# One pool for the four 4 MiB buffers at the end of a decode-attention kernel

## The chip, the cores and the metric

One core of a Trainium2 chip. The metric is the device time of one execution in microseconds (us). The kernel before takes 1310.4 us (median of 4 executions, 1310.23 to 1310.52). The profile of one execution spans 1308.8 us; its times count from the start of that span. A run on one core has no second die to be compared with; every profiled run here counts as undisturbed ("fast").

## The reference, cut to what matters

```python
# A: one decode step of attention.   B, D = 8, 576;  H, Sk, Dh = 32, 4096, 128
q = (x @ wq).reshape(B, 1, H, Dh).transpose(0, 2, 1, 3)
scores = einsum("bhqd,bhkd->bhqk", q, k_cache) * Dh ** -0.5      # k_cache: 256 MiB in bf16
o = einsum("bhqk,bhkd->bhqd", softmax(scores), v_cache)          # v_cache: 256 MiB in bf16
a = o.transpose(0, 2, 1, 3).reshape(B, 1, H * Dh) @ wo
# B: layernorm, 576 -> 4608 -> 576 MLP with gelu, small.   g = sigmoid((x * gate_w).sum(-1))
return g * a + (1 - g) * b
```

All of K and V has to be read once. That and some 20 MB of weights make 557 MB.

## The kernel before, where the change touches it

The work is cut into NG = 64 groups of 4 heads and one batch row. For each group VectorE multiplies K by q, TensorE sums the products to scores, and after the softmax TensorE multiplies the weights by V (the PV product); ScalarE then copies (evicts) that product from TensorE's accumulators, and two small groups of matmuls, gather and total, add up its parts and the softmax sums. A group needs one K tile and one V tile of 4 MiB, each 128 partitions of 128 key positions by 128 elements. K has two buffers, V has two; a tile of group g goes into buffer g % 2 when the tile of g - 2 has been used. The tiles below are named by group: K 62, V 63 and so on; V 63 is the last and comes in seven pieces. All loads are issued in order by one queue, SP, which stops at a load that has to wait.

```python
KB = [sb(f"KB{i}", [128, NTT, DH], BF16) for i in range(2)]
VB = [sb(f"VB{i}", [128, NTT, DH], BF16) for i in range(2)]
...
def load_k(g):                       # waits for the last VectorE product with K of group g - 2
    s = g % 2
    nK[s] += 1
    src = kv_src(A_k_cache, g)
    k_land[g] = op("sync", lambda e: e.dma_start(KB[s][:, :, :], src), [k_done.get(g - 2)], dma=(sK[s], 16 * nK[s]))
# load_v(g): the same with VB, v_done: the PV product of group g - 2 on TensorE
V_LAST = (32, 32, 16, 16, 16, 8, 8)
def load_v_pieces(g):                # V 63, piece by piece, each with its own semaphore
    ...
    t = load("sync", dst, part, f"sVl{n}", [v_done.get(g - 2)])
...
for g in range(NG):
    if 1 <= g <= NG - 3:
        load_k(g + 1)
    if 1 <= g <= NG - 2 and g != NG - 3:
        load_v(g)
    def between(c, g=g):             # called between the four score chunks of group g
        if c == 1 and g >= 1:
            rowsum(g - 1)
            if g < NG - 1:
                ...
            else:                    # group 63
                pv(NG - 3, 0, 1)     # PV of group 61: 32 matmuls
                evict(NG - 3)
                load_v_pieces(g)     # V 63 goes where V 61 was
        ...
        if c == 3:
            if 1 <= g < NG - 2:
                pv(g - 1, 0, 1)
                evict(g - 1)
    scores(g, between)               # VectorE products with K, TensorE sums, VectorE reductions
    if g == NG - 3:
        load_k(g + 2)                # K 63, after K 61 has been used
        load_v(g)
    ...
    softmax(g)
# after the loop: PV of 62, then PV of 63 piece by piece, normalisation, output projection, output
```

## Time and profile before

| what | value | view |
|---|---|---|
| DMA, mean over the span | 426 GB/s | the page, DMA packets |
| DMA share of the chain that ended last | 69% | the page, part 4 |
| VectorE, TensorE busy | 66%, 64% | the page, part 1 |
| V 63 issued | 1289.53 us | timeline of the SP queue |
| last data landed | 1304.68 us | chain in order of time |

Three lines of the page, each slice 32.7 us long: the mean busy share of the 16 DMA engines in tenths, what they moved, and the whole.

```profile
DMA  9999999999999999999999999999999999999997
GB/s 398 422 431 432 431 432 431 432 431 430 434 424 432 430 431 429 428 418 432 429 431 429 431 431 431 431 432 430 432 430 431 431 431 429 432 431 432 429 420 311
DMA packets 25255, 557.77 MB, mean 426 GB/s; under 512 B 2528, under 2 KB 6640, under 8 KB 7536
```

The kernel streams at about 431 GB/s in most slices. The end is the only slice that falls far short, and the last 4 us of it are the tail of arithmetic after the last byte. The windows view of the end (busy time of the engines by stretch; the last three columns are TensorE's granted clock, the DMA share and GB/s) shows a hole before that tail:

```profile
1280.00:1284.00 4.00, 1.40 (x4) 0.58 (x5) 3.97 (x4) 2.30 (x4) 0.00 (x0) 0.76 1.03 442
1284.00:1288.00 4.00, 4.00 (x22) 1.45 (x24) 3.38 (x4) 0.00 (x0) 0.00 (x0) 0.81 0.91 393
1288.00:1292.00 4.00, 3.61 (x38) 1.37 (x31) 4.00 (x4) 0.60 (x1) 0.00 (x0) 1.00 0.66 256
1292.00:1296.00 4.00, 3.67 (x40) 2.18 (x42) 2.26 (x9) 0.38 (x1) 0.00 (x0) 1.00 0.96 395
1296.00:1300.00 4.00, 2.84 (x53) 2.32 (x45) 0.69 (x1) 2.52 (x5) 0.00 (x0) 0.90 0.99 395
1300.00:1304.00 4.00, 3.35 (x85) 3.16 (x85) 0.54 (x3) 0.00 (x0) 0.00 (x0) 0.50 0.64 245
```

The waits of the SP queue (total us, times, longest us) name the cause, and its timeline gives the moments. The first two lines are the ordinary waits for a buffer, through the whole kernel; the third is the one before V 63:

```profile
SPq L223 <- DVE p L354: 950.5, 60, 26.3
SPq L229 <- PE psb L346: 215.1, 58, 4.2
...
SPq L187 <- PE psb L414: 28.8, 1, 28.8
```

```profile
1236.99 19.95 SPq L223 DMA_DIRECT2D KB<-in_A_k_cache_dram  x2
1256.98 3.77 SPq L229 DMA_DIRECT2D VB<-in_A_v_cache_dram  x2
1289.53 3.77 SPq L187 DMA_DIRECT2D VB<-in_A_v_cache_dram  x7
```

The reader sees K 62 and K 63 (issued 20 us apart), V 61 and V 62, and then 28.8 us in which the queue waits for the PV product of group 61 (L414) before it may issue V 63. The chain in order of time ends with the landing of V 63 and a short tail:

```profile
1292.80 11.88 DMA VB<-in_A_v_cache_dram
1304.68 0.05 issue
1304.72 0.39 PE psb L508 x8
1305.11 0.02 issue
1305.14 0.19 DVE OT_sb L517
```

The page does not show what each of the 16 DMA engines does, but the trace can be read for it. It holds 16 landing records for each of these loads, read here as one for each engine (the prediction below says on what ground). This table is worked out from those records (us; "7th" and "8th" in order of landing). The records do not name the engines: "the last engine" is the one that lands last.

```
kernel before   first     7th      8th      last    spread
first K tile      -        -        -        -       0.52
K 62           1256.56  1258.23  1263.59  1264.74    8.18
K 63           1268.16  1268.90  1273.31  1274.46    6.30
V 61           1277.87  1278.61  1283.02  1284.17    6.30
V 62           1287.58  1288.32  1292.71  1294.69    7.11
V 63, piece 1  1294.25  1294.73  1295.20  1297.15    2.90
V 63, piece 7  1302.09  1302.56  1302.77  1304.68    2.58
```

Seven engines are ahead and nine are behind. Those ahead land a tile every 9.71 us unless nothing has been issued; so do those behind, except that the last one needed 10.5 us for V 62. What an engine still has queued is called its ring below; an engine with nothing queued has run dry. From V 62 to the end the first engine takes 14.5 us and the last 10.0 us.

### The profile page before, as it was taken

The numbers are of one execution on the slowest core, as the hardware profiler recorded it, in microseconds if no ns is written. First come the engines' busy times: TensorE is split into PE (matmuls) and PEld (weight loads), VectorE is DVE, ScalarE is ACT, GpSimd is POOL, SyncE is SP. The second block draws the span as 40 slices with busy tenths as digits, with TensorE's granted clock in tenths as the row PEclk, the third lists the DMA queues.
The fourth block names the chain that finished last, engine by engine and source line by source line (L and its number), as shares of the span: only waits on it lengthen the run. The fifth ranks groups of instructions, "written<-read, shape, count | busy, mean of one in ns | idle before, by whom it ended". The sixth has DMA issues, their size and how long they took to land.

```text
span 1308.8 us, 12641 instructions
## 1 busy us (share of the span) xinstructions
PE 843.5 (64%) x5428; PEld 384.4 (29%) x5428; DVE 869.7 (66%) x1061; ACT 204.1 (16%) x393; POOL 2.5 (0%) x13
## 2 busy tenths in 40 slices
PE   3567766766746666646766766765766665766766
PEld 1223433433312233212322222322322222322323
DVE  4576676676747667646766766766776666776675
ACT  1201111111210110101011111011111111111111
POOL 0000000000000000000000000000000000000000
PEclk8878888878868888768878878878878878878878
DMA  9999999999999999999999999999999999999997
GB/s 398 422 431 432 431 432 431 432 431 430 434 424 432 430 431 429 428 418 432 429 431 429 431 431 431 431 432 430 432 430 431 431 431 429 432 431 432 429 420 311
DMA packets 25255, 557.77 MB, mean 426 GB/s; under 512 B 2528, under 2 KB 6640, under 8 KB 7536
## 3 DMA queue, kind: packets, MB, share of 16 engines
q1 hardware_dynamic: 24944, 556.95, 99.4%
q8 instruction: 42, 0.69, 0.2%
q14 instruction: 13, 0.11, 0.0%
q10 hardware_dynamic: 256, 0.03, 0.0%
HBM read 556.96 MB, written 0.01 MB: 426 GB/s over the span
## 4 chain that ended last, share of the span: by engine, by line
DMA 69%; DVE 20%; PE 10%; SPq 0%; issue 0%; ACT 0%
DMA KB<-in_A_k_cache_dram 68%; DVE p L354 16%; PE psb L364 10%; DVE s_sb L369 3%; DMA VB<-in_A_v_cache_dram 1%; SPq L187 0%; PE psb L414 0%; ACT L467 0%; SPq L229 0%; DVE mA L387 0%; SPq L223 0%; PE psb L477 0%; DVE mB L389 0%; ACT O_sb L427 0%; DVE gm L390 0%
## 5 line engine op out<-in xcount | busy, mean ns | idle before, releaser
L364 PE MATMUL psb<-p,ident 128*128 128x512 bf16 x2048 | 610.9, 459 | 412.2 <-DVE p L354 411.8
L354 DVE TENSOR_TENSOR p<-KB,q_bc 128x4096 bf16<-128x4096 bf16 x256 | 579.6, 2285 | 278.0 <-DMA KB<-in_A_k_cache_dram 278.0
L364 PEld LDWEIGHTS psb<-p,ident 128*128 128x128 bf16 x2048 | 218.1, 114 | 744.5 <-DVE p L354 445.2
L369 DVE TENSOR_REDUCE s_sb<-psb 128x32 f32<-128x512 f32 x256 | 176.1, 688 | 129.9 <-PE psb L364 129.6
L427 ACT ACTIVATE O_sb<-psb 128x512 f32<-128x512 f32 x63 | 37.6, 597 | 1032.2 <-PE psb L414 1032.2
L396 ACT ACTIVATE P<-s_sb,mD 32x128 bf16<-32x128 f32 x256 | 147.0, 574 | 12.9 <-DVE mD L393 9.0
L414 PE MATMUL psb<-VB,P 128*16 128x512 bf16 x2016 | 119.9, 379 | 0.3 <-DMA VB<-in_A_v_cache_dram 0.3
L432 PE MATMUL psb<-sel,O_sb 128*128 128x4 f32 x504 | 66.9, 256 | 32.9 <-ACT O_sb L427 32.9
L432 PEld LDWEIGHTS psb<-sel,O_sb 128*128 128x128 f32 x504 | 61.6, 192 | 41.3 <-ACT O_sb L427 41.2
L414 PEld LDWEIGHTS psb<-VB,P 128*16 128x16 bf16 x2016 | 44.7, 89 | 70.4 <-issue 26.3
L402 DVE TENSOR_REDUCE rs<-P 128x4 f32<-128x512 bf16 x64 | 43.5, 680 | 2.1 <-ACT P L396 2.1
L421 PEld LDWEIGHTS psb<-rs,ones 128*128 128x128 f32 x128 | 24.4, 192 | 9.3 <-issue 0.4
L348 ACT ACTIVATE q_bc<-psb 128x128 bf16<-128x128 f32 x64 | 17.4, 272 | 32.7 <-PE psb L346 32.7
L452 PEld LDWEIGHTS psb<-yT_sb,RB 128*128 128x128 bf16 (+1 forms) x216 | 19.4, 165 | 3.4
L452 PE MATMUL psb<-yT_sb,RB 128*128 128x8 bf16 (+1 forms) x216 | 19.8, 227 | 0.0
L387 DVE TENSOR_REDUCE mA<-s_sb 128x1 f32<-128x128 f32 x64 | 18.3, 286 | 2.2
L421 PE MATMUL psb<-rs,ones 128*128 128x4 f32 x128 | 18.4, 214 | 0.0
L389 DVE STREAM_TRANSPOSE mB<-mA 128x32 f32<-128x32 f32 x64 | 13.6, 213 | 2.2
L393 DVE STREAM_TRANSPOSE mD<-mC 128x32 f32<-128x32 f32 x64 | 13.6, 212 | 2.2
L346 PE MATMUL psb<-Q,Sel 128*128 128x128 bf16 x64 | 14.7, 229 | 0.0
L346 PEld LDWEIGHTS psb<-Q,Sel 128*128 128x128 bf16 x64 | 6.1, 96 | 27.0 <-issue 26.8
L390 DVE TENSOR_REDUCE gm<-mB 128x1 f32<-128x32 f32 x64 | 11.9, 186 | 2.2
(63 smaller groups left out, 84.7 us busy)
## 6 DMA issues: line engine op xcount, KB each, us to landing
KB<-in_A_k_cache_dram SPq DMA_DIRECT2D x64, 4096.0 KB, 27.2
VB<-in_A_v_cache_dram SPq DMA_DIRECT2D x63, 4096.0 KB, 33.1
RB<-in_B_w_dram SPq DMA_DIRECT2D x1, 5184.0 KB, 44.3
RB<-in_B_w_dram SPq DMA_DIRECT2D x1, 4608.0 KB, 36.6
RB<-in_A_wo_dram SPq DMA_DIRECT2D x1, 4608.0 KB, 44.7
RB<-in_A_wq_dram SPq DMA_DIRECT2D x1, 4096.0 KB, 12.8
VB<-in_A_v_cache_dram SPq DMA_DIRECT2D x2, 1024.0 KB, 8.7
VB<-in_A_v_cache_dram SPq DMA_DIRECT2D x3, 512.0 KB, 11.2
```

Of the source, the lines that this page charges most:

```text
L346: t = op("tensor", lambda e: e.matmul(qb_ps[:, 0:DH], lhsT=Sel[:, b, :], rhs=Q4[:, hg * DH:(hg + 1) * DH], start=True, stop=True), [a_Q[hg ...
L354: v_mult[g, c] = op("vector", lambda e: e.tensor_tensor(out=p1[:, par, :, :], in0=KB[s][:, c * CT:(c + 1) * CT, :], in1=qb, op=ALU.mult), ...
L364: p_sum[g, c] = op("tensor", lambda e, r=r, n=n: e.matmul(tr_ps[par][:, :], lhsT=ident[:, :], rhs=r, start=(n == 0), stop=(n == NCH - 1)), w)
L369: v_red[g, c] = op("vector", lambda e: e.tensor_reduce(out=s_sb[:, s, c * CT:(c + 1) * CT], in_=tr_ps[par][:, :].rearrange("p (t c) -> p t ...
L387: t = op("vector", lambda e: e.tensor_reduce(out=mA[:, 0:1], in_=s_sb[:, s, :], axis=AX.X, op=ALU.max), [v_red[g, NCK - 1], c_mA])
L396: a_exp[g] = op("scalar", lambda e, h=h, q=q: e.activation(out=P[q, s, :, h], in_=s_sb[q, s, :], func=ACT.Exp, bias=mD[q, s, 0:1], scale=1.0),
L402: v_rs[g] = op("vector", lambda e: e.tensor_reduce(out=rs[:, s, :], in_=P[:, s, :, :].rearrange("p t h -> p h t"), axis=AX.X, op=ALU.add), ...
L414: p_pv[g] = op("tensor", lambda e, o=o, tq=tq: e.matmul(o, lhsT=P[:, s, tq * TQ:(tq + 1) * TQ, :].rearrange("p t h -> p (t h)"), rhs=VB[s] ...
L421: p_z[g] = op("tensor", lambda e: e.matmul(oz_ps[:, HB:2 * HB], lhsT=ones[:, :], rhs=rs[:, g % 2, :], start=True, stop=True), [v_rs[g], v_ ...
L427: a_ev[g] = op("scalar", lambda e: e.activation(out=O_sb[:].rearrange("p t d -> p (t d)"), in_=o_ps[s][:, :], func=ACT.Copy), [p_pv[g], p_ ...
L432: p_oz[g] = op("tensor", lambda e, tt=tt: e.matmul(oz_ps[:, 0:HB], lhsT=O_sb[:, tt, :], rhs=sel16[:, tt, :], start=(tt == 0), stop=(tt == ...
L452: st["p_up"] = op("tensor", lambda e, w=w, o=o, kt=kt: e.matmul(o, lhsT=w, rhs=yT_sb[:, kt, :], start=(kt == 0), stop=(kt >= NKF)), [*ld_w ...
```

## The change

Its intent: no transfer near the end should wait for a late product. The four buffers become one pool. K 63 goes where V 59 was, V 61 where K 61 was, and V 63 where K 62 was, whichever came free first. The order of the loads stays; the PV product of group 61 no longer holds back V 63 and moves on TensorE behind all score sums of group 63.

```diff
-    KB = [sb(f"KB{i}", [128, NTT, DH], BF16) for i in range(2)]
-    VB = [sb(f"VB{i}", [128, NTT, DH], BF16) for i in range(2)]
+    KV = [sb(f"KV{i}", [128, NTT, DH], BF16) for i in range(4)]
...
+    k_slot = {g: g % 2 for g in range(NG)}
+    v_slot = {g: 2 + g % 2 for g in range(NG)}
+    k_slot[NG - 1], v_slot[NG - 3], v_slot[NG - 1] = 3, 1, 0
+    free = [None] * 4
...
+    def load_tile(cache, g, i):
+        nS[i] += 1
+        src = kv_src(cache, g)
+        return op("sync", lambda e: e.dma_start(KV[i][:, :, :], src), [free[i]], dma=(sS[i], 16 * nS[i]))
...     (all uses of KB, VB, k_done, v_done become KV, k_slot, v_slot, free)
     for g in range(NG):
         if 1 <= g <= NG - 3:
             load_k(g + 1)
+        if g == NG - 3:
+            load_k(g + 2)
+        if g == NG - 1:
+            load_v_pieces(g)
...
-                else:
-                    pv(NG - 3, 0, 1)
-                    evict(NG - 3)
-                    load_v_pieces(g)
...
             if c == 3:
+                if g == NG - 1:
+                    pv(g - 2, 0, 1)
+                    evict(g - 2)
...
         if g == NG - 3:
-            load_k(g + 2)
             load_v(g)
```

More of the change, by code (lines that the diff above doesn't have):

```diff
@@ L180, in bass_gated_mix__mha_block_cached__mixer_channel_mlp__decode_kernel @@
     YT_COL = 64
-    sK = [nc.alloc_semaphore(f"sK{i}") for i in range(2)]
-    sV = [nc.alloc_semaphore(f"sV{i}") for i in range(2)]
-    nK, nV = [0, 0], [0, 0]
+    sS = [nc.alloc_semaphore(f"sS{i}") for i in range(4)]
+    nS = [0] * 4
+    k_slot = {g: g % 2 for g in range(NG)}
+    v_slot = {g: 2 + g % 2 for g in range(NG)}
+    k_slot[NG - 1], v_slot[NG - 3], v_slot[NG - 1] = 3, 1, 0
+    free = [None] * 4
     def load(engine, dst, src, name, waits=()):
@@ L214, in kv_src @@
         return cache[b, hg * HB:(hg + 1) * HB].rearrange("h (p t) d -> (h p) t d", p=32)
-    k_done, v_done = {}, {}
     k_land, v_land = {}, {}
+    def load_tile(cache, g, i):
+        nS[i] += 1
+        src = kv_src(cache, g)
+        return op("sync", lambda e: e.dma_start(KV[i][:, :, :], src), [free[i]], dma=(sS[i], 16 * nS[i]))
     def load_k(g):
-        s = g % 2
-        nK[s] += 1
-        src = kv_src(A_k_cache, g)
-        k_land[g] = op("sync", lambda e: e.dma_start(KB[s][:, :, :], src), [k_done.get(g - 2)], dma=(sK[s], 16 * nK[s]))
+        k_land[g] = load_tile(A_k_cache, g, k_slot[g])
     def load_v(g):
-        s = g % 2
-        nV[s] += 1
-        src = kv_src(A_v_cache, g)
-        t = op("sync", lambda e: e.dma_start(VB[s][:, :, :], src), [v_done.get(g - 2)], dma=(sV[s], 16 * nV[s]))
-        v_land[g] = [(t, 0, NTT)]
+        v_land[g] = [(load_tile(A_v_cache, g, v_slot[g]), 0, NTT)]
     V_LAST = (32, 32, 16, 16, 16, 8, 8)
     def load_v_pieces(g):
-        s = g % 2
+        i = v_slot[g]
         src = kv_src(A_v_cache, g)
@@ L239, in load_v_pieces @@
         for n, nt in enumerate(V_LAST):
-            dst, part = VB[s][:, t0:t0 + nt, :], src[:, t0:t0 + nt, :]
-            t = load("sync", dst, part, f"sVl{n}", [v_done.get(g - 2)])
+            dst, part = KV[i][:, t0:t0 + nt, :], src[:, t0:t0 + nt, :]
+            t = load("sync", dst, part, f"sVl{n}", [free[i]])
             v_land[g].append((t, t0, t0 + nt))
@@ L354, in mult @@
         v_mult[g, c] = op("vector", lambda e: e.tensor_tensor(
-            out=p1[:, par, :, :], in0=KB[s][:, c * CT:(c + 1) * CT, :], in1=qb, op=ALU.mult),
+            out=p1[:, par, :, :], in0=KV[k_slot[g]][:, c * CT:(c + 1) * CT, :], in1=qb, op=ALU.mult),
             [k_land[g], a_qb[g], p_sum.get((g, c - 2) if c >= 2 else (g - 1, c + NCK - 2))]
@@ L358, in mult @@
         if c == NCK - 1:
-            k_done[g] = v_mult[g, c]
+            free[k_slot[g]] = v_mult[g, c]
         for n in range(NCH):
@@ L415, in pv @@
                     o, lhsT=P[:, s, tq * TQ:(tq + 1) * TQ, :].rearrange("p t h -> p (t h)"),
-                    rhs=VB[s][:, tq * TQ:(tq + 1) * TQ, :].rearrange("p t d -> p (t d)"),
+                    rhs=KV[v_slot[g]][:, tq * TQ:(tq + 1) * TQ, :].rearrange("p t d -> p (t d)"),
                     start=(tq < 4), stop=(tq >= NTQ - 4)), w)
-        v_done[g] = p_pv[g]
+        free[v_slot[g]] = p_pv[g]
     def total(g):
@@ L508, in pv_turned @@
                 p_oz[g] = op("tensor", lambda e, t=t: e.matmul(
-                    o_ps[s][:, 0:HB], lhsT=VB[s][:, t, :], rhs=P[:, s, t, :], start=(t == 0), stop=(t == NTT - 1)),
+                    o_ps[s][:, 0:HB], lhsT=KV[v_slot[g]][:, t, :], rhs=P[:, s, t, :], start=(t == 0), stop=(t == NTT - 1)),
                     [land, a_exp[g], a_ev.get(g - 2)] if t == t0 else ())
```

## The prediction

> **What bounds the kernel.** The sixteen DMA engines: the page's slices show DMA at 9 tenths or more in 39 of 40 slices, 426 GB/s on average over the 1308.8 us span; the chain of waits is 69% DMA. A 4 MiB tile takes 9.71 us (8 packets of 32 KB per engine, 1.215 us each). VectorE (66%) and TensorE (64%) have room.
>
> **What the change is after.** In the windows view DMA falls to 393 and 256 GB/s between 1284 and 1292 us. The SP queue's waits show why: the last V, in seven pieces, waits 28.8 us for the PV product of group 61 and is issued at 1289.5 us. The last K is late too (1256.6 us). After the change the last K waits for an older PV product, done near 1240.8 us, and the last V for the last product with K 62, done near 1276.5 us: 13 us earlier, so no engine's ring runs dry. No bytes or issues are removed. On TensorE PV 61 (1.9 us) moves behind the score sums of group 63.
>
> Read naively, the hole is worth about 4.5 us.
>
> **Why I expect almost nothing.** The Trainium skill ("DMA: Bandwidth & Descriptors", on why a DMA increments its semaphore by 16) says that the engines of one DMA finish independently. The trace agrees: each tile has 16 landing events, whose spread grows from 0.5 us at the start to 8.2 us near the end. For V 62, seven land at 1288.0 to 1288.7, nine at 1293.1 to 1295.1 us; for the last piece all land between 1302.5 and 1305.1. So the hole is idleness of engines that are ahead: 14.5 us from V 62 to the end for one tile. The last engine takes 10.0 us, and the pieces' packets on one engine sum to 10.1 us (16 of 0.309, 24 of 0.159, 16 of 0.084): its ring never ran dry, and it decides when the last piece lands, which the final PV waits for. With a fixed share per engine, an earlier issue lets the early engines finish near 1298 us and moves the last one by nothing. The late last K likewise costs only early engines (1.9 us).
>
> **The tail.** After the last landing: 8 small matmuls, normalisation, 16 matmuls, output, about 4 us, unchanged. Before it, PV 61, its eviction and gather now follow the score sums, so the work up to the last pieces may run about 1 us later (1.9 + 0.6 + 1.0 us, against less waiting for V 62). TensorE had gaps of 0.7 and 0.3 us before the last pieces, which absorb most of it: an estimated 0 to 0.4 us lost. An instruction fetch of 1.1 us that falls on another DMA engine could move the end by 0.7 us either way.
>
> **Prediction:** 1310.4 us, 8 in 10 between 1308.6 and 1311.5. Faster by over 2%: 0.01; within 2%: 0.98; slower by over 2%: 0.01.
>
> **What would show it right:** the last V's pieces issued near 1276.5 us, the last K near 1241 us; no fall of throughput at 1284 to 1292, but a longer one at the end (from about 1298 on, some engines only); the last piece's landing events spread over 6 to 8 us instead of 2.6; the last landing within 1 us of 1304.7. Wrong: last landing 3 to 5 us earlier with a small spread.
>
> **What would make it wrong:** if shares are not fixed and idle engines take over work; if late engines run faster or slower by what others do; if the queue takes fewer outstanding transfers than now stand in it; or if the reordered TensorE work at the end, under a clock granted at 0.5, becomes the critical path (1 to 2 us).

One correction to its numbers: the landing times of single engines in it are 0.4 us too late throughout, because the landing records had been lined up with the span's start by eye. Differences between them are not touched. The tables here are lined up exactly. The same shift is in the 1295.1 us of e4's expectation, and it fits the 1.4 to 1.5 us from issue to first packet that e2 to e4 count with (1.0 in the tables).

## The result, and the profile after

| | before | after |
|---|---|---|
| median us (executions) | 1310.4 (4) | 1310.37 (4) |
| range us | 1310.23 to 1310.52 | 1310.2 to 1310.51 |
| span of the profiled run | 1308.8 | 1308.7 |
| V 63 issued | 1289.53 | 1276.54 |
| last data landed | 1304.68 | 1304.55 |

The ratio is 1.0, with a 95% interval of 0.9982 to 1.0017. The time is the same, and so is the throughput (the same lines of the page as before the change):

```profile
GB/s 396 424 431 432 431 431 431 432 430 431 434 425 430 431 431 430 426 420 431 430 428 429 430 432 431 431 432 431 431 431 431 431 430 428 432 432 430 432 431 300
DMA packets 25255, 557.77 MB, mean 426 GB/s; under 512 B 2528, under 2 KB 6640, under 8 KB 7536
```

Yet the change did what it was made for. The SP queue's waits and timeline of the kernel after:

```profile
SPq L190 <- DVE p L354: 16.2, 1, 16.2
```

```profile
1237.09 4.14 SPq L224 DMA_DIRECT2D KV<-in_A_k_cache_dram  x2
1256.18 4.14 SPq L224 DMA_DIRECT2D KV<-in_A_v_cache_dram  x2
1276.54 3.18 SPq L190 DMA_DIRECT2D KV<-in_A_v_cache_dram  x7
```

K 63 is now issued within 4 us of K 62, and V 63 13 us earlier, behind a VectorE product. The windows view of the kernel after shows that the hole is gone from 1284 to 1292 us and has come back later, at 1296 to 1304 us:

```profile
1280.00:1284.00 4.00, 1.32 (x4) 0.50 (x5) 3.94 (x4) 2.30 (x4) 0.00 (x0) 0.58 1.03 442
1284.00:1288.00 4.00, 4.00 (x12) 1.49 (x11) 3.11 (x4) 0.00 (x0) 0.00 (x0) 0.56 1.00 422
1288.00:1292.00 4.00, 2.57 (x12) 0.80 (x9) 4.00 (x4) 0.00 (x0) 0.00 (x0) 1.00 0.95 401
1292.00:1296.00 4.00, 3.73 (x40) 1.42 (x40) 2.38 (x8) 0.15 (x1) 0.00 (x0) 1.00 0.93 379
1296.00:1300.00 4.00, 3.50 (x60) 2.37 (x61) 1.05 (x3) 3.34 (x6) 0.00 (x0) 1.00 0.58 238
1300.00:1304.00 4.00, 3.82 (x111) 3.64 (x109) 0.54 (x3) 0.03 (x1) 0.00 (x0) 1.00 0.42 165
```

And the end of the chain of the kernel after, where 25 us of the DMA piece have taken the place of 12, ends at the same moment:

```profile
1279.29 25.27 DMA KV<-in_A_v_cache_dram
1304.55 0.05 issue
1304.60 0.39 PE psb L508 x8
1304.99 0.02 issue
1305.01 0.19 DVE OT_sb L517
```

The landing records say where the hole went:

```
kernel after    first     7th      8th      last    spread
K 62           1256.79  1258.38  1263.56  1265.03    8.24
K 63           1266.49  1268.09  1273.28  1274.75    8.26
V 61           1276.20  1277.81  1282.99  1284.46    8.26
V 62           1285.92  1287.52  1292.73  1294.61    8.69
V 63, piece 1  1288.39  1289.99  1295.21  1297.08    8.69
V 63, piece 7  1296.02  1297.59  1302.67  1304.55    8.53
```

Now no engine pauses. The seven that are ahead finish V 63 between 1296.0 and 1297.6 us instead of near 1302.3 us, and have nothing more to do. The last engine lands V 62 and V 63 at 1294.61 and 1304.55 us, as before (1294.69 and 1304.68).

### The profile page after: what moved, and what is told of

The parts are those of the page before. It is cut to its first block, busy times and chain, and to the rows that moved or that the text cites. A ratio compares the mean times of both kernels' runs of the same rounds, so it can differ in the third digit from the quotient of the medians.

```text
span 1308.7 us, 12641 instructions
## 1 busy us (share of the span) xinstructions
PE 842.2 (64%) x5428; PEld 383.3 (29%) x5428; DVE 869.8 (66%) x1061; ACT 204.1 (16%) x393; POOL 2.5 (0%) x13
## 4 chain that ended last, share of the span: by engine, by line
DMA 70%; DVE 20%; PE 9%; SPq 0%; issue 0%; ACT 0%
DMA KV<-in_A_k_cache_dram 68%; DVE p L354 16%; PE psb L364 9%; DVE s_sb L369 3%; DMA KV<-in_A_v_cache_dram 2%; SPq L190 0%; PE psb L414 0%; SPq L224 0%; ACT L467 0%; PE psb L477 0%; ACT O_sb L427 0%; DVE mA L387 0%; DVE hT_sb L468 0%; ACT up L467 0%; DVE mB L389 0%
## 5 line engine op out<-in xcount | busy, mean ns | idle before, releaser
L354 DVE TENSOR_TENSOR p<-KV,q_bc 128x4096 bf16<-128x4096 bf16 x256 | 579.6, 2285 | 279.1 <-DMA KV<-in_A_k_cache_dram 279.1
L414 PE MATMUL psb<-KV,P 128*16 128x512 bf16 x2016 | 119.9, 379 | 0.0
L414 PEld LDWEIGHTS psb<-KV,P 128*16 128x16 bf16 x2016 | 44.7, 89 | 69.9 <-issue 26.3
L390 DVE TENSOR_REDUCE gm<-mB 128x1 f32<-128x32 f32 x64 | 11.9, 186 | 2.2
```

The lines of the kernel that those rows point to most:

```text
L354: v_mult[g, c] = op("vector", lambda e: e.tensor_tensor(out=p1[:, par, :, :], in0=KV[k_slot[g]][:, c * CT:(c + 1) * CT, :], in1=qb, op=ALU ...
L414: p_pv[g] = op("tensor", lambda e, o=o, tq=tq: e.matmul(o, lhsT=P[:, s, tq * TQ:(tq + 1) * TQ, :].rearrange("p t h -> p (t h)"), rhs=KV[v_ ...
```

## The experiments

**Theory A**: every DMA engine has a fixed share of each transfer; only the engine furthest behind sets the end, and its ring never ran dry before the change either. **Rival B**: the earlier issue did gain time, and the later PV 61 on TensorE gave it back. **Rival C**: engine time idle anywhere counts, so the mean over the 16 engines decides. **Rival D** (to a second part of A, why an engine falls behind): instruction fetches are hidden. Medians of all runs, each against the kernel before on the same chip in the same rounds:

| run | us, median (range) | before beside it | ratio, 95% interval |
|---|---|---|---|
| e1_pool_only | 1310.51 (1310.23 to 1310.72) | 1310.62 | 0.9999, 0.9983 to 1.0016 |
| e2_gate_before_knee | 1312.08 (1311.97 to 1312.26) | 1310.62 | 1.0012, 0.9997 to 1.0027 |
| e3_gate_after_knee | 1318.95 (1318.43 to 1319.25) | 1310.62 | 1.0063, 1.0048 to 1.0078 |
| e4_order_only | 1315.33 (1315.1 to 1315.82) | 1310.62 | 1.0037, 1.0022 to 1.0052 |
| e5_uneven_share | 1316.24 (1316.12 to 1316.97) | 1310.6 | 1.0044, 1.0028 to 1.0061 |
| e6_more_fetches | 1314.95 (1314.9 to 1315.06) | 1310.6 | 1.0033, 1.0018 to 1.0048 |
| e7_gate_fetch_moved | 1319.34 (1319.25 to 1319.61) | 1310.74 | 1.0065, 1.0052 to 1.0079 |
| e8_fewer_fetches | 1309.89 (1309.61 to 1309.99) | 1310.74 | 0.9993, 0.998 to 1.0007 |
| e9_uneven_strided | 1316.05 (1315.75 to 1316.39) | 1310.6 | 1.0041, 1.0026 to 1.0057 |
| e10_fewer_fetches_old_pools | 1310.44 (1310.3 to 1311.2) | 1310.6 | 0.9999, 0.9987 to 1.0012 |

All gave correct results. The argument uses differences of 0.1 to 0.7%, read beside the executions of one kernel in one round, which lie within 1 us, and beside the landings in the traces. Apart from e1, the interval holds 1 in e2, e8 and e10 (in e2 and e8 no execution overlaps with those of before, in e10 they do).

### e1_pool_only: the pool, with PV 61 at its old place

```diff
# against the kernel after
                     total(g - 1)
+                else:
+                    pv(g - 2, 0, 1)
+                    evict(g - 2)
...
-                if g == NG - 1:
-                    pv(g - 2, 0, 1)
-                    evict(g - 2)
```

> The pool and the early issues of the change, but PV 61 at its old place on TensorE (behind the first two score chunks of group 63). Theory A (each DMA engine has a fixed share, and only the engine that is furthest behind sets the end; its ring never ran dry before the change either): 1310.3 us, within 0.4 us of both kernels; last landing near 1304.7 us. Rival B (the earlier issue did gain 1 to 4 us, and the later PV 61 on TensorE gave it back): 1306 to 1309 us.

Measured: 1310.51 us, last landing 1304.63 us. Rival B falls: nothing was gained that TensorE could have given back.

### e2, e3, e4: the issue of V 63 at other moments

e2_gate_before_knee and e3_gate_after_knee hold the pieces of the kernel after back until a chosen instruction; e4_order_only is the TensorE half of the change on the old buffers, which holds them back too.

```diff
# e2, against the kernel after (load_v_pieces gets one more wait, "gate")
-        if g == NG - 1:
-            load_v_pieces(g)
...
         if g == NG - 1:
+            load_v_pieces(g, v_red[g, 2])     # third score reduction of group 63
# e3: the call stands after the loop instead
     evict(last - 1)
+    load_v_pieces(last, p_pv[last - 1])       # PV of group 62
# e4, against the kernel before: PV 61, its eviction and load_v_pieces move from c == 1 to c == 3
```

> The changed kernel, with the pieces of the last V held back until the third score reduction of group 63, so issued near 1292.7 us instead of 1276.5; first packet 1.4 us later, near 1294.1 us. The last engine ends V 62 near 1294.7 us. Theory A: no time lost, 1310.4 us within 0.5, although the hole in DMA throughput becomes larger than before the change (seven engines idle for some 7 us). Rival C (idle time counts as the mean over the 16 engines, that is as bytes not moved): 7 engines x 7.6 us / 16 = 3.3 us more, 1313.7 us.

> The same, held back until PV 62 is done, near 1299.4 us; first packet near 1300.8 us. Now every ring runs dry. Theory A: later by 1300.8 minus 1294.7, 6.1 us: 1316.5 us within 0.8, and the landing spread of the last piece falls below 1.5 us as all engines start together. Rival C: mean idle (7 x 14.4 + 9 x 7.5) / 16 = 10.5 us more, 1320.9 us.

> The kernel before with only the TensorE move of the change: PV 61 behind all score sums of group 63. Its buffer holds back the last V, so the pieces are issued near 1295.8 us, first packet near 1297.3 us, against 1295.1 us when the last engine ends V 62. Theory A: 2.2 us more than before, 1312.6 us within 0.7. Rival C: (7 x 6.3 + 9 x 3) / 16, some 4.4 us more, 1314.8 us.

Measured, with the moments from the traces (us; "piece 1" and "piece 7" are the landings on the last engine):

```
          issue of V 63  first packet  V 62 last  piece 1   piece 7   fetch in V 63  time
after        1276.54       1285.37     1294.61    1297.08   1304.55     1302.6      1310.37
before       1289.53       1290.56     1294.69    1297.15   1304.68     1301.9      1310.4
e2           1292.23       1293.20     1294.45    1297.10   1306.09     1303.6      1312.08
e4           1295.76       1296.73     1294.29    1300.43   1309.35     1304.2      1315.33
e3           1299.26       1300.22     1294.25    1303.97   1312.82     1309.0      1318.95
```

The column "piece 1" is the sharp test. Issue V 63 at 1276.5, 1289.5 or 1292.2 us, and the last engine lands the first piece at 1297.1 us all the same (in e2 it had landed V 62 0.2 us sooner, so up to 0.2 us may be lost there). Issue it at 1295.8 or 1299.3 us and it lands 3.3 or 6.9 us later. Between lies a knee, at the moment when the last engine would run dry, and the kernel before stood in front of it. Behind the knee the delay is passed on whole: the first packet of e3 comes 3.5 us after that of e4, and so does the landing of piece 1. The windows view of e2 shows how big a hole may be in front of the knee without moving piece 1:

```profile
1284.00:1288.00 4.00, 3.94 (x13) 1.34 (x11) 3.45 (x4) 0.00 (x0) 0.00 (x0) 0.70 0.65 274
1288.00:1292.00 4.00, 2.24 (x10) 0.91 (x11) 4.00 (x4) 0.00 (x0) 0.00 (x0) 1.00 0.51 221
1292.00:1296.00 4.00, 3.39 (x40) 1.19 (x37) 1.97 (x7) 0.56 (x1) 0.00 (x0) 1.00 0.72 250
```

Both A and C missed the totals, and the last piece's spread in e3 was 1.63 us where A said below 1.5. Theory A's two terms need a correction each. First, the restart was mis-sized. A dry engine needs 3.7 us from its first packet to the landing of piece 1 (e3: 1300.22 to 1303.97), but a fed one lands piece 1 2.5 us after V 62, so the knee for the first packet lies about 1.2 us before the last landing of V 62, near 1293.4 us. Second, in e2, e3 and e4 all engines run V 63 side by side (spread 0.4 to 0.6 us), and then one of them drops back by 1.2 to 1.4 us just after a 16 KB instruction fetch, whose time is the column "fetch": in e2 it moves from the pack (second to last 1304.79 us) to 1306.09 us. Both terms were found after the runs and from them, so their sums show that nothing large is missing, not more. With both terms the sums are 6.9 + 1.3 = 8.2 us for e3 (measured 8.3 above its runs of before), 3.3 + 1.4 = 4.7 us for e4 (4.7), and 0 + 1.3 = 1.3 us for e2 (1.5). C happened to be close in e4 alone (4.4 against 4.7); it is 1.8 us too high in e2 and 2.2 us too high in e3, and it does not give the flat column.

### e6_more_fetches: more instructions where TensorE waits anyway

The second term asks why an engine is behind at all. In the traces the lags of the engines grow in steps. The Trainium skill ("Runtime: NRT & Kernel Launch", Instruction fetch mechanics) says that each compute engine refills its instruction memory in blocks of 16 KiB, 256 instructions, over a DMA queue, and that the cost of crossing a block is "mostly hidden". The trace agrees on the size: 42 packets of 16 KB, of 1.07 us (median), in the kernel before, and 28 more for the 7168 instructions that e6 adds. The page's words are about the engine that runs the instructions; whether the fetches are hidden from the DMA engines that carry the data was tested by adding instructions.

```diff
# against the kernel after, behind gather(g - 1)
+        if 1 <= g <= 56:
+            for _ in range(64):
+                op("tensor", lambda e, g=g: e.matmul(o_ps[(g - 1) % 2][0:16, 0:4], lhsT=ident[:, 0:16],
+                                                     rhs=ident[:, 0:4], start=True, stop=True), [c_id])
```

> The changed kernel with 64 tiny matmuls more (and their weight loads) on TensorE in each of 56 groups, at a place where TensorE then waits for the next K anyway; results unused. That is 7168 instructions, 28 blocks of 16 KB more to fetch (42 before). Theory A with its second part (each fetch of a block sets one DMA engine back by about 1.5 us, and these set-backs make the engine that is last): shared over 9 to 16 engines, 1.7 to 3.1 blocks each, 2.6 to 4.8 us more: 1313 to 1315.2 us, with a larger spread of landings near the end. Rival D (the fetches are hidden and the spread has another origin): 1310.4 us and the spread of 8.5 us as it was. If TensorE became the limit instead, the waits of VectorE for K landings would vanish.

Measured: 1314.95 us, 4.4 us above its runs of before (4.6 above the kernel after); last landing 1308.94 instead of 1304.55 us; spread near the end 11.7 to 11.9 us instead of 8.5. The page's line of the instruction queue (packets, MB, share), first after, then e6:

```profile
q8 instruction: 42, 0.69, 0.2%
```

```profile
q8 instruction: 70, 1.15, 0.4%
```

VectorE's wait for K (total, times, longest) shows that TensorE did not become the limit; again first after, then e6:

```profile
DVE p L354 <- DMA KV<-in_A_k_cache_dram: 279.1, 62, 15.9
```

```profile
DVE p L354 <- DMA KV<-in_A_k_cache_dram: 283.1, 62, 15.9
```

The landing records count the steps. For every tile, sum how far the 15 other engines land behind the first, and follow that sum over 67 tiles in the middle, where only K and V are loaded:

```
                 from tile at  to tile at  16 KB fetches  8 KB fetches  sum of lags, us   steps over 0.7 us  all other steps together
kernel before       596.2        1237.1         20             6         31.8 to 69.0           24               0.4 us
e6_more_fetches     597.6        1238.6         35             6         35.3 to 96.2           38               1.4 us
```

In the kernel before, 24 of the 66 steps hold nearly the whole growth, and their number is close to that of the fetches (two that fall into one tile make one step). The moments agree too: each of the 24 steps, and of the 38 in e6, has a fetch between the first landing of the tile before it and the last of its own, and the 25 tiles of the kernel before with no fetch there have no step. The growth is that of the nine engines behind: in this stretch of the kernel before, the 7th landing goes from 0.9 to 1.7 us behind the first, the 8th from 2.4 to 5.5. The 18 steps between 1.2 and 1.9 us have a median of 1.57 us: that is what one block takes from one engine. With 15 fetches more the sum grows by 24 us more, 1.6 us each. In this stretch the fetches are the lag.

28 blocks more cost 4.4 us: 0.16 us a block. Of the 4.4 us at the last landing, 3.2 are a larger lag behind the first engine (11.69 against 8.53 us); by the other 1.2 us the first engine itself is later, which it is already at the first tile of the stretch, and what did that was not followed. Rival D falls. The extra matmuls also kept TensorE busy for 97.8 us more; the unchanged wait for K is what speaks against that as the cause.

### e7_gate_fetch_moved: e3 with the last fetch shifted

```diff
# against e3, behind gather(g - 1)
+        if 1 <= g <= 50:
+            for _ in range(2):
+                op("tensor", ...)             # the tiny matmul of e6
```

> The kernel of e3_gate_after_knee (last V held back until PV 62), with 100 tiny matmuls more on TensorE, two in each of 50 early groups, so that the last instruction fetch, which came at 1309.2 us in the middle of the last V and set one engine back by 1.3 us, comes near 1299 us, when every ring is dry. The first part of the loss in e3 (7.0 us from the late restart) stays, the second (1.3 us) goes: theory A with fetches 1317.7 us, within 0.4, and the last piece's landing spread below 0.6 us. If the set-back of the one engine has another cause than the fetch, 1318.95 us and the spread of 1.6 us as in e3. If a further fetch falls into the last V all the same, which the trace will show, the run decides nothing.

Measured: 1319.34 us. A fetch fell into V 63 all the same, at 1310.9 us instead of 1309.0 us, so by its own terms the run decides nothing about the total. It does show one thing: the set-back moved with the fetch. In e3 the spread jumps from 0.43 to 1.66 us between pieces 4 and 5; here it stays at 0.37 to 0.39 us up to piece 6 and jumps to 1.77 us at piece 7.

### e5_uneven_share and e9_uneven_strided: moving bytes between engines

If shares are fixed by how a DMA is cut, a DMA of 8 rows should load eight engines only. The Trainium skill ("DMA: Bandwidth & Descriptors", Why a DMA increments its semaphore by 16 and not by 1) says that the largest number up to 16 that divides the slowest dimension is taken, and the lowest-numbered engines. 24 of the 128 positions of V 63 were loaded in this way.

```diff
# against e1_pool_only
-    V_LAST = (32, 32, 16, 16, 16, 8, 8)
+    V_LAST = (24, 32, 16, 16, 16, 8, 8, 8)
...
+            if n == 0:
+                lead = nc.alloc_semaphore("sVlead")
+                for j in range(16):           # e9: rows b, b + 4, ..., b + 28 instead of eight adjacent ones
+                    dst, part = KV[i][8 * j:8 * j + 8, 0:nt, :], src[8 * j:8 * j + 8, 0:nt, :]
+                    t = op("sync", lambda e, dst=dst, part=part: e.dma_start(dst, part), [free[i]], dma=(lead, 256))
```

> The pool with PV 61 at its old place, and 24 of the 128 positions of the last V loaded by sixteen DMAs of 8 rows each, that the Trainium skill says run on the lowest-numbered eight engines (one row each); the other 104 positions over all sixteen as before. No byte more or less. Engines 8 to 15 get 1.8 us less work in the last tile, engines 0 to 7 1.8 us more. Theory A: if the engines that are ahead are among the first eight, the last landing falls from 1304.7 to near 1302.9 us and the time to 1308.6 us (within 0.7); if an engine that is far behind is among them, the last landing rises by 1.8 us, to 1312.2 us. Rival C (mean throughput decides): no change, 1310.4 us. The eight landing events of each of these DMAs show which case it is.

> As e5_uneven_share, but the eight rows of each of the sixteen DMAs are four partitions apart instead of adjacent. In e5 the 6 KB packets of these DMAs took a median of 0.36 us, the fastest 0.234 us, and the run lost 5.7 us where 1.8 were expected. The Trainium skill (SBUF, the DMA port swizzle) says that four adjacent partitions share a port; eight rows four apart reach eight ports. If ports were what slowed e5: packets near 0.234 us and a time near 1312 us (three of the first eight engines are among those behind, which adds 1.8 us to the 1310.4). If the slowing has another cause (the queue, or the mere number of DMAs): packets near 0.36 us again and 1316 us.

Measured: 1316.24 and 1316.05 us. Each of these DMAs left nine landing records, one at issue and eight later, so eight engines took part; which eight the records do not say. They were the wrong ones: in e5, 80 of the 128 landings came by 1294 us and 48 from 1296 us on, which, at 16 landings an engine, is five engines that were ahead and three that were behind. That turns the expected gain into a loss, as the expectation allowed, but of 5.6 and 5.5 us instead of 1.8. In e5 the 6 KB packets took a median of 0.36 us instead of 0.234. In e9 the packets to partitions 0 to 63, which come first, took 0.234 us, and most of those to partitions 64 to 127 about 0.46 us; the nine engines that are behind landed V 62 1.7 us later than in the kernel after (2.5 us in e5), while the others wrote their extra rows. The Trainium skill ("SBUF — State Buffer", The DMA port swizzle) says that partitions 64 to 127 lie on other ports than 0 to 63, and "DMA: Bandwidth & Descriptors" (The descriptor swizzle) that engines 8 to 15 write them in a load of 128 rows. Sharing of ports fits this, but no run isolates it. Neither outcome that was expected of e9 came as a whole: the packets were fast at first, and the time did not fall.

What follows: in neither run was the idle time of the engines ahead turned into a gain; with extra load on engines that are behind the loss was larger than that load (1.8 us), and what made the rest stays open.

### e8 and e10: fewer fetches

If fetches make the laggards, fewer instructions should help. With bf16 operands the gather and total matmuls run once instead of twice: 632 TensorE instructions fewer.

```diff
# e8: against the kernel after;  e10: the same edit against the kernel before
# cut: the block is opened under nc.allow_low_precision
-    ones = sb("ones", [128, 128], F32)
-    sel16 = sb("sel16", [128, TQ, HB], F32)
-    rs = sb("rs", [128, 2, HB], F32)
-    O_sb = sb("O_sb", [128, TQ, DH], F32)
+    ones = sb("ones", [128, 128], BF16)       # and sel16, rs, O_sb likewise
```

> The changed kernel with the evicted PV product, the selector, the row sums and the ones in bf16 instead of fp32, so that the gather and total matmuls run in one pass instead of two: 316 matmuls and as many weight loads fewer, 632 instructions, 2.5 blocks of 16 KB less to fetch. Theory A with fetches, by the slope of e6 (4.5 us for 28 blocks, 0.16 us a block): 0.4 us less than the changed kernel, 1310.0 us; a set-back more or less on the one last engine may hide it (0.7 us either way). Rival D (fetches hidden): 1310.4 us or, if the shorter tail on TensorE counts, 1310.0 too; the landing spread tells them apart.

> The kernel before with the bf16 edit of e8 alone, without the common pool. Theory A: the pool is worth nothing, so 1309.9 us as e8, within 0.5; the fetches fall from 42 to 40. If the pool has a worth that only shows when the last engine is less far behind, e10 is 1 us or more slower than e8 was against its own runs of before (0.85 us faster).

Measured: e8 1309.89 us, 0.85 below its runs of before, with 40 fetches; last landing 1303.72 us. All its executions (1309.61 to 1309.99) are below all of before on that chip (1310.39 to 1311.31), but the interval of the ratio still holds 1. The gain does not come from the arithmetic after the last landing: that landing is 0.83 us earlier than in the kernel after, and the spread of the last piece is 7.90 us instead of 8.53. e10 1310.44 us, 0.16 below its runs of before, also 40 fetches; last landing 1304.32 us. In e10 the last engine landed V 62 at 1293.55 us, earlier than in e8 (1293.76), but piece 1 came 3.25 us later instead of 2.48, and a fetch stands at 1295.8 us. So which engine a late fetch falls on may be worth as much as the whole edit; that this and not the pool makes the 0.6 us between e8 and e10 is argued, not shown. Neither outcome expected of e10 came: it is a little above 1309.9 us ± 0.5, and its gain is 0.7 us short of e8's, not 1 us or more. A small worth of the pool, once the last engine is less far behind, is not excluded. e8 has the lowest median here, by less than 0.1% and not clear of noise.

## Why the prediction was right

- *"What bounds the kernel"*: 426 GB/s before and after, in both cases with the last landing some 4 us before the end. Right.
- *The issue times*: V 63 was predicted near 1276.5 us and issued at 1276.54; the last K near 1241 us, and the issues of the two K loads (1237.09, 4.14 us long) end at 1241.23. All seven pieces were issued within 3.2 us, so the queue took them. Right.
- *"the hole is idleness of engines that are ahead"*: shown by e2. With a hole much larger than before the change, the first piece landed on the last engine at 1297.10 us, against 1297.08 after and 1297.15 before. For the late K 63 it shows in the tables: before the change the spread fell from 8.18 to 6.30 us at K 63, but the last engine landed it at 1274.46 us, after the change at 1274.75.
- *"moves the last one by nothing"*: 1304.68 to 1304.55 us. The spread of the last piece grew from 2.58 to 8.53 us; predicted 6 to 8, since the engines ahead came to rest a little earlier (1296.0 to 1297.6 us) than "near 1298".
- *The tail*: PV 61, its eviction and gather did move the work of TensorE back; the third piece's products began at 1302.29 us after and 1301.67 before, and that was absorbed in waits for data. e1, with the old order, takes the same time.
- *"if late engines run faster or slower by what others do"*: not in the kernels before and after. But the same worry came true in e5 and e9.
- *The instruction fetch*, put down as a chance of 0.7 us either way, was undersized: one sets an engine back by 1.2 to 1.4 us when all run side by side, and fetches make the lag that made the change worthless, nearly all of its growth in the stretch that was counted. That this did not move the result is chance: the last engine shows no step at the fetch of 1302.6 us, and in the kernel before the fetch at 1301.9 us set an engine back to within 0.01 us of the last one (piece 6: 2.61 and 2.62 us behind the first). The mechanism was predicted; the agreement of the median to 0.03 us is in part luck.

What stays open: which engine each fetch runs on (the records don't name it), what makes the lag outside the stretch that was counted, and whether e8's gain over e10 would last.

## What to carry to other kernels

When a stream of loads fills the DMA engines, do not price a hole in the mean throughput by its area: look at the landing of each engine, and ask whether the last one ever ran dry. In this kernel an earlier issue was worth the time by which the last engine had been dry, and nothing before that knee. What puts an engine last, here in large part the instruction fetches of a long unrolled program, may then be a better target than the order of the loads; two of 42 fetches fewer gained 0.85 us at most here, which is not clear of noise.

## What the Trainium skill lacked or had wrong

- "Runtime: NRT & Kernel Launch", Instruction fetch mechanics: the cost of crossing a 16 KiB boundary is called "mostly hidden". That is said of the engine that runs the instructions; what a fetch takes from a stream of loads is not priced. In this kernel, limited by DMA, a fetch packet takes 1.07 us and adds a median of 1.57 us to the lags, and 28 fetches more cost 4.4 us.
- "DMA: Bandwidth & Descriptors": it says that the engines of a DMA finish independently, but not that in a long stream the lag accumulates. Here the spread of the landings of one 4 MiB load grew from 0.52 to 8.2 us, and idle engines did not take over work (8.5 us idle at the end).
- The same page, Latency and other measured facts, gives about 0.6 us to the first byte of a load issued by SP, without saying from when it counts. Here it took 1.0 us from the start of the issuing instruction to the first packet when some or all rings were empty (1289.53 to 1290.56, 1292.23 to 1293.20, 1299.26 to 1300.22), 0.6 to 0.7 us from its end (it lasts 0.33 us), and 3.7 us more to the landing of a 1 MiB piece.
- The same page has no figure for a load cut so that eight engines write rows of all 128 partitions while the others still write theirs: in e9 most 6 KB packets to partitions 64 to 127 took about 0.46 us instead of 0.234.
